# Sliding-window attention and SwiGLU block on one core: first values shifted half by DMA, two sums and the next keys issued at other places

## The chip, the core and the metric

The kernel runs on one core of one Trainium2 chip. The metric is the device time of one execution in microseconds (us). Before the change three runs took 337.42 us in the median (337.41 to 337.79).

## What is computed

Attention over a causal window of 64 positions, for 8 batches of 8 heads with 576 positions and head size 64; its output, 4608 tokens of 512 numbers, goes through a gated feed-forward block of width 1536.

```python
scores = scale * np.matmul(q, k.transpose(0, 1, 3, 2))      # 8 x 8 x 576 x 576
mask = (rel >= 0) & (rel < window)                          # window = 64
attn = softmax(where(mask, scores, -1e9))
x = np.matmul(attn, v).transpose(0, 2, 1, 3).reshape(4608, 512)
g = x @ w_gate                                              # 512 x 1536
silu = g * (1.0 / (1.0 + np.exp(-g)))
val = x @ w_val
return (silu * val @ w_out).astype(np.float32)              # 1536 x 512
```

Inputs and output are float32; the kernel multiplies in bf16.

## The kernel before, in words

The tokens are cut into nine tiles of 512 (t = 0 to 8). Tiles 0 to 6 and 8 are the first 512 positions of a batch; tile 7 gathers the last 64 positions of all eight. A tile passes through four stages.

- Scores (`scores`, L201): for each pair u of heads, small matmuls of 64 keys with the queries that can see them; `Exp` on ScalarE (L233) makes the weights E. For t = 0 the mask is added by matmuls with a bias (L219), later VectorE multiplies E with it (L235).
- Values: `totals` (L243) sums E with a matrix of ones into d_ps; ScalarE forms the inverse as exp(-log(d)), `log` at L253 and `invert` at L256. `values` (L265) multiplies E with v, 16 matmuls for a pair (L271), and VectorE scales the result into xT (L277).
- Gate (`gate_value`, L302): twelve steps m, each with eight matmuls of 512 columns (L306) into g_ps and v_ps; `gate_end` (L294) does silu on ScalarE (L299) and the product hT on VectorE (L300). For t = 0 the first two steps are done piece by piece by `gate_part` (L283, matmuls at L286), since each quarter c needs only the values of pair c.
- Projection (`project_part`, L312): twelve quarters of hT with wo (L315) into o_ps; VectorE copies it and SP stores it (L322, L325). Projection of tile t stands between the scores and values of tile t + 1.

The window of a 64-key block reaches over the boundary between two chunks of 128 positions. So v is kept twice: v1 has the chunks as they are, and v2 is shifted by 64 rows, with lower and upper half each on its own partitions. `shift_v` (L150) fills v2 from v1 with two copies per call: L155 copies the upper halves, L156 the lower. Its argument `copy` says who does it. For t = 0 it is called twice, for the chunks 0 and 1 and for 2 and 3, both times with VectorE (`on_v`). `values` takes v2 for even blocks and v1 for odd ones, in the order m = 0 to 7, so the first half of a pair's sixteen matmuls needs chunks 0 and 1, the second half chunks 2 and 3. For t >= 2 the shift is done with `shift_dma` (L401): SP starts a DMA from v1 to v2.

The order of the work is written out by hand: each engine executes its instructions in the order of the program text, and waits for what it reads. Around the change, it is this.

- Loads. SP starts the raw q and k of batch 0 and half of its v, ScalarE two quarters of k (L351 to L357). GpSimd starts everything that changes its type on the way: v chunks 2 and 3 of batch 0 (L430), the gate weights in five pairs (L442 to L447), q of batch 1 (L448, tile q_s), wo in three parts (L449 to L451), v of batch 1. Batch 1's keys are loaded raw (k_f) in four quarters by ScalarE's queue, L502, one after each of the gate steps m = 3 to 6. ScalarE casts a quarter (`join`, L505, instruction at L408) after the silu of m = 7 to 10, TensorE transposes it after the gate step m = 8 to 11 (L509, instruction at L174), and VectorE copies the result to kT (L510, instruction at L177). `turn_q` (L182, instruction at L186) turns batch 1's queries on VectorE, after m = 10, m = 11 and the loop.
- `keep_warm` (L366) issues matmuls on a tile of ones whose result nobody reads, seven at the start and a few later, six after `scores(0, 3)`.
- `log_of` (L465) does the sums and the log of one pair. Those of pairs 0 and 1 are done together (L455 to L460); pair 2's stand after the values of pairs 0 and 1, pair 3's between the two halves of the first gate pieces (L471 to L478).

Of the kernel before, what the change touches and what calls it, by code (L numbers as in the profile page):

```python
# [8 lines left out]
P = 128  # L9
# [8 lines left out]
def kernel(  # L18
# [10 lines left out]
    nc = tc.nc  # L29
    S, D, H = 576, 64, 8  # L30
# [23 lines left out]
    ones = cst.tile([P, 512], BF16, name="ones")  # L54
# [17 lines left out]
    def load_runs(eng, dst, src, t, hs):  # L72
        eng.dma_start(
            dst.rearrange("r h e d -> r h (e d)"),
            src[batch(t), hs, 0:512].rearrange("h (r e) d -> r h (e d)", e=4),
        )
# [73 lines left out]
    def shift_v(t, copy, lo=0, hi=4):  # L150

        a, b = v1[t % 2], v2[t % 2]
        top = min(hi, 3)
        if top > lo:
            copy(b[64:128, lo + 1:top + 1], a[64:128, lo:top])  # L155
        copy(b[0:64, lo:hi], a[0:64, lo:hi])  # L156
# [14 lines left out]
    def transposes(tp, src):  # L171

        for e in range(4):
            nc.tensor.transpose(tp[:, P * e:P * e + P], src[:, e], identb[:])  # L174

    def split_k(dst, tp):
        nc.vector.tensor_copy(  # L177
            dst.rearrange("p (r e) -> p r e", e=4),
            tp.rearrange("p (e r) -> p r e", e=4),
        )  # L180

    def turn_q(t, u):  # L182

        if u == 0:
            queries[t] = att.tile([P, 4, 512], BF16, name="qT", tag="qT")
        nc.vector.transpose(  # L186
            queries[t][:, u, :].rearrange("r (e x) -> r e x", e=16),
            staged[t][0][:, u].rearrange("r (e d) -> r e d", d=D)[:, :, 0:32],
        )
# [53 lines left out]
    def totals(t, u, d_ps):  # L243
        for h in range(2):
            nc.tensor.matmul(  # L245
                d_ps[64 * h:64 * h + 64], ones[:, 0:D], weights[t, u][:, h, :]
            )

    def room(n):
        return fsb.tile([P, 2, 512], FP32, name="r", tag="r", bufs=4)[:, 0:n]  # L250

    def log(r, d_ps):
        nc.scalar.activation(r, d_ps, AF.Ln)  # L253
# [11 lines left out]
    def values(t, u, o_ps):  # L265
        E = weights.pop((t, u))
        if u == 0:
            xT[t] = att.tile([P, 4, 512], BF16, name="xT", tag="xT")
        for m in range(8):
            for h in range(2):  # L270
                nc.tensor.matmul(  # L271
                    blocks(o_ps[64 * h:64 * h + 64], t, m, m + 1),
                    (v1, v2)[m // 4][t % 2][:, m % 4, 2 * u + h, :] if t == LAST
                    else (v2, v1)[m % 2][t % 2][:, m // 2, 2 * u + h, :],
                    blocks(E[:, h, :], t, m, m + 1),
                )
        nc.vector.tensor_mul(xT[t][:, u, :], o_ps[:], inverse.pop((t, u)))  # L277
# [5 lines left out]
    def gate_part(t, ms, tiles, c):  # L283
        for m, pair in zip(ms, tiles):
            for ps, w in zip(pair, (wg, wv)):
                nc.tensor.matmul(  # L286
                    ps[:], w[:, c, P * m:P * m + P], xT[t][:, c, :],
                    start=(c == 0), stop=(c == 3),
                )

    def gate_tiles():
        return [ps_f.tile([P, 512], FP32, name=x + "_ps", tag=x) for x in "gv"]

    def gate_end(t, m, pair):  # L294
        if m == 0:
            hT[t] = hpool.tile([P, 12, 512], BF16, name="hT", tag="hT")
        g_ps, v_ps = pair
        sg = fsb.tile([P, 512], FP32, name="sg", tag="sg")
        nc.scalar.activation(sg[:], g_ps[:], AF.Silu)  # L299
        nc.vector.tensor_mul(hT[t][:, m, :], sg[:], v_ps[:])  # L300

    def gate_value(t, m):  # L302
        pair = gate_tiles()
        for ps, w in zip(pair, (wg, wv)):
            for c in range(4):
                nc.tensor.matmul(  # L306
                    ps[:], w[:, c, P * m:P * m + P], xT[t][:, c, :],
                    start=(c == 0), stop=(c == 3),
                )
        gate_end(t, m, pair)  # L310
# [33 lines left out]
    def set_exp():  # L344
        nc.scalar.preload_act_table_set("natural_log_exp_and_others")
# [7 lines left out]
    for u in range(4):  # L353
        hs = slice(2 * u, 2 * u + 2)
# [1 line left out]
        load_runs(nc.scalar if u < 2 else nc.sync, raw[1][:, hs], k, 0, hs)  # L356
    load_v(nc.sync, staged[0, "v"], 0, (0, 1))  # L357
    set_exp()
    nc.vector.memset(ones[:], 1.0)
    make_identity(nc, identb[:])  # L360
    nc.vector.memset(zero[:], 0.0)
    for i in range(2):
# [1 line left out]
    warm = ps_f.tile([P, 512], FP32, name="warm", tag="v")  # L364

    def keep_warm(n):  # L366
        for _ in range(n):
            nc.tensor.matmul(warm[0:D], ones[:, 0:D], ones[:])

    keep_warm(7)  # L370
    nc.gpsimd.memset(tri[:], 1.0)
    for a in range(2):
        half = tri[64 * a:64 * a + 64]
# [25 lines left out]
    on_v, on_p, on_a = nc.vector.tensor_copy, nc.gpsimd.tensor_copy, nc.scalar.copy  # L399
# [7 lines left out]
    def join(copy, dst, src):  # L407
        copy(dst.rearrange("r e (h d) -> r h e d", h=2), src)  # L408

    def one(name):  # L410
        return ps_a.tile([P, 2, 512], FP32, name=name, tag="a")[:, 0]
# [48 lines left out]
    invert(r)  # L460
    scores(0, 3)
    shift_v(0, on_v, 0, 2)
    shift_v(0, on_v, 2, 4)

    def log_of(u):  # L465
        d_ps = one("d_ps")
        totals(0, u, d_ps)
        inverse[0, u] = room(1)[:, 0]
        log(inverse[0, u], d_ps)

    keep_warm(6)  # L471
    for u in range(2):
        values(0, u, ps_f.tile([P, 512], FP32, name="ao_ps", tag="gv"[u])[:])
    log_of(2)
    pairs = [gate_tiles() for _ in range(2)]
    gate_part(0, (0,), pairs, 0)
    log_of(3)
    gate_part(0, (1,), pairs[1:], 0)  # L478
    for u in (2, 3):
        invert(inverse[0, u])  # L480
    values(0, 2, one("ao_ps"))
# [6 lines left out]
    for m in range(12):  # L488
        if m < 2:
            gate_end(0, m, pairs[m])  # L490
        else:
            gate_value(0, m)
        if m == 2:
            for i in range(4):
                nc.vector.tensor_copy(
                    mask[:, 0, :, i], tri[:].rearrange("r c (x e) -> r e c x", e=16)
                )
            nc.vector.memset(mask[64:128, 0, :, 0, 0, :], 0.0)
            nc.vector.tensor_copy(mask[:, 1], mask[:, 0])
        if 3 <= m < 7:  # L500
            hs = slice(2 * m - 6, 2 * m - 4)
            load_runs(nc.scalar, raw_k[:, hs], k, 1, hs)  # L502
        if 7 <= m < 11:
            u = m - 7
            join(on_a, keys[:, u], raw_k[:, 2 * u:2 * u + 2])  # L505
        if m >= 8:
            u = m - 8
            tp = ps_a.tile([P, 512], BF16, name="tp", tag="a")
            transposes(tp, keys[:, u])  # L509
            split_k(kT[1][:, u, :], tp[:])  # L510
        if m >= 10:
            turn_q(1, m - 10)
    turn_q(1, 2)
    turn_q(1, 3)

    set_exp()
# [96 lines left out]
```

The softmax here doesn't subtract the row's maximum and nothing guards it: scores larger than these inputs give would overflow.

## Time and profile before

| | |
|---|---|
| median of three runs | 337.42 us |
| the profiled execution | 337.54 us, span 335.7 us |
| TensorE busy | 323.2 us, 96% of the span |
| VectorE, ScalarE, GpSimd busy | 214.2, 169.2, 137.8 us |
| first values (L271) | 13.93; second half of pair 0 from 14.99 |
| first gate matmul (L286) | 16.16 |
| first matmul of the gate step m = 2 (L306) | 21.29 |
| batch 1's scores, pair 0 and pair 1 (L227) | 39.94, 42.02 |
| first projection matmul (L315) | 42.38 |
| batch 1's first gate matmul (L306) | 56.29 |

Times in the lower rows are microseconds from the start of the span. The page gives each engine's busy time; the span in 40 slices of 8.4 us, with tenths of busy time for each engine and for the 16 DMA engines; and the DMA queues, of which q0 carries what GpSimd starts, q1 what SP starts and q10 what ScalarE starts. The chain of waits follows the work that ended last back from the end, and lists what released each step. The list of waits says for which releaser an engine stood idle. A window of the DMA view counts the packets of each queue in that stretch. A DMA's landing is the moment at which its semaphore tells that all of it is there.

### The profile page before, as it was taken

Reading aid. Unit: us, or ns where it says so; the run is one execution under the profiler, and the core shown is the slowest. Engines: PE = TensorE matmul, PEld = TensorE weight load, DVE = VectorE, ACT = ScalarE, POOL = GpSimd, SP = SyncE. Lnnn points to the kernel's source line nnn. Section 1 sums busy time; section 2 is a strip of 40 time slices with the busy share of each in tenths; the row PEclk is TensorE's granted clock in tenths of the full one; section 3 lists DMA queues with packets and bytes.
Section 4 is the critical chain, followed back from the end, with each engine's and each line's share of the span. In section 5 each row is a group of like instructions: output and inputs, shape, how many; then the busy total and the mean of one; then the engine's idle time right before and its main releaser. Section 6 shows DMA issues by size and latency. Waiting matters only on the chain.

```text
span 335.7 us, 6932 instructions
## 1 busy us (share of the span) xinstructions
PE 323.2 (96%) x2683; PEld 153.9 (46%) x2729; DVE 214.2 (64%) x318; ACT 169.2 (50%) x241; POOL 137.8 (41%) x247
## 2 busy tenths in 40 slices
PE   8899799999999999999999999999999999999994
PEld 3444344444544454445444544444444444544441
DVE  5754766588667756785678656865786476753431
ACT  4764656336733763366435553565347633763300
POOL 5944345946767965256123896163200000000000
PEclk9999999999999999999999999999999999999999
DMA  7999999999899499639931999199401320010013
GB/s 261 205 202 226 229 188 223 125 205 215 147 248 186 52 176 234 124 58 209 185 89 20 170 180 167 12 189 177 111 0 48 79 56 3 23 72 31 3 32 94
DMA packets 83057, 44.12 MB, mean 131 GB/s; under 512 B 63824, under 2 KB 77648, under 8 KB 83024
## 3 DMA queue, kind: packets, MB, share of 16 engines
q0 software_dynamic: 49328, 22.56, 54.2%
q1 hardware_dynamic: 31680, 19.02, 20.6%
q10 hardware_dynamic: 2016, 2.10, 2.2%
q8 instruction: 21, 0.34, 0.4%
q14 instruction: 12, 0.10, 0.1%
HBM read 54.00 MB, written 9.44 MB: 189 GB/s over the span
## 4 chain that ended last, share of the span: by engine, by line
PE 88%; DMA 6%; DVE 3%; issue 2%; ACT 1%; DVEq 0%
PE g_ps L306 26%; PE v_ps L306 26%; PE o_ps L315 25%; PE s_ps L227 3%; DMA k_f<-in_k_dram 3%; PE ao_ps L271 3%; PE d_ps L245 3%; DMA q_f<-in_q_dram 1%; PE tp L174 1%; PE g_ps L286 1%; ACT E L233 1%; DVE kT L177 1%; PE v_ps L286 1%; DMA out_dram<-os__4409 1%; DMA out_dram<-os__4428 1%
## 5 line engine op out<-in xcount | busy, mean ns | idle before, releaser
L299 ACT ACTIVATE sg<-g_ps 128x512 f32<-128x512 f32 x108 | 64.4, 597 | 112.1 <-PE g_ps L306 79.9
L300 DVE TENSOR_TENSOR hT<-sg,v_ps 128x512 bf16<-128x512 f32 x108 | 74.9, 694 | 62.9 <-PE v_ps L306 59.9
L306 PE MATMUL v_ps<-xT,wv 128*128 128x512 bf16 x417 | 108.3, 379 | 0.5
L306 PE MATMUL g_ps<-xT,wg 128*128 128x512 bf16 x413 | 107.6, 379 | 0.5
L315 PE MATMUL o_ps<-wo,hT 128*128 128x512 bf16 x405 | 96.5, 380 | 1.6 <-issue 0.6
L107 POOL DMA_DIRECT2D k_s<-in_k_dram x112 | 60.7, 551 | 29.8 <-DMA q_s<-in_q_dram 20.5
L306 PEld LDWEIGHTS <-wv 128*128 128x128 bf16 x424 | 41.5, 98 | 50.0
L306 PEld LDWEIGHTS <-wg 128*128 128x128 bf16 x424 | 41.4, 98 | 49.5 <-issue 0.3
L315 PEld LDWEIGHTS <-hT 128*128 128x128 bf16 x432 | 39.6, 98 | 45.1 <-issue 0.4
L233 ACT ACTIVATE E<-s_ps 128x1024 bf16<-128x1024 f32 x36 | 35.2, 1021 | 8.4 <-PE s_ps L227 8.2
L277 DVE TENSOR_TENSOR xT<-ao_ps,r 128x512 bf16<-128x512 f32 x36 | 24.7, 691 | 22.7 <-ACT r L256 20.5
L196 DVE STREAM_TRANSPOSE kT<-k_s 128x512 bf16<-128x512 bf16 x28 | 35.9, 1284 | 0.0
L253 ACT ACTIVATE r<-d_ps 128x512 f32<-128x512 f32 (+1 forms) x35 | 21.0, 601 | 22.4 <-PE d_ps L245 22.4
L235 DVE TENSOR_TENSOR E<-E,mask 128x1024 bf16<-128x1024 bf16 x28 | 20.5, 739 | 11.5 <-ACT E L233 11.5
L87 POOL DMA_DIRECT2D q_s<-in_q_dram x28 | 15.3, 558 | 26.7 <-DVE qT L186 16.0
L148 POOL CAST v<-v_f 128x512 bf16<-128x512 f32 x22 | 14.3, 665 | 21.5 <-DMA v_f<-in_v_dram 17.5
L256 ACT ACTIVATE r<-r 128x512 f32<-128x512 f32 (+1 forms) x35 | 22.3, 641 | 1.1
L186 DVE STREAM_TRANSPOSE qT<-q_s 128x512 bf16<-128x512 bf16 x32 | 22.3, 702 | 0.0
L271 PEld LDWEIGHTS <-v 128*64 128x64 bf16 x576 | 13.8, 112 | 5.7 <-issue 1.7
L271 PE MATMUL ao_ps<-E,v 128*64 128x64 bf16 x576 | 15.3, 196 | 0.6 <-DVE v L156 0.6
L245 PE MATMUL d_ps<-E,ones 128*64 128x512 bf16 x72 | 13.9, 392 | 0.3
L227 PE MATMUL s_ps<-qT,kT 64*64 64x128 bf16 (+1 forms) x640 | 12.5, 211 | 0.2 <-DVE kT L177 0.2
(95 smaller groups left out, 175.6 us busy)
## 6 DMA issues: line engine op xcount, KB each, us to landing
q_s<-in_q_dram POOLq DMA_DIRECT2D x28, 248.0 KB, 6.7
k_s<-in_k_dram POOLq DMA_DIRECT2D x112, 56.0 KB, 5.2
v_f<-in_v_dram SPq DMA_DIRECT2D x22, 256.0 KB
v<-in_v_dram POOLq DMA_DIRECT2D x18, 128.0 KB, 4.8
k_f<-in_k_dram ACTq DMA_DIRECT2D x6, 256.0 KB
wo<-in_moe_w_out_dram POOLq DMA_DIRECT2D x3, 512.0 KB, 16.0
v<-v SPq DMA_DIRECT2D x6, 256.0 KB
v<-v SPq DMA_DIRECT2D x6, 192.0 KB
```

Source lines behind the costliest of these rows:

```text
L107: nc.gpsimd.dma_start(k_s[p0:p0 + 32, g, :, 0:w], k[b, a:H:2, s:s + P].rearrange("u (r e) d -> r u (e d)", e=4) [:, :, 32 * c:32 * c + w],)
L186: nc.vector.transpose(queries[t][:, u, :].rearrange("r (e x) -> r e x", e=16), staged[t][0][:, u].rearrange("r (e d) -> r e d", d=D)[:, :, ...
L196: nc.vector.transpose(dst[:, u, :].rearrange("r (g x e) -> r g e x", g=4, e=4), k_s[:, :, u].rearrange("r g (e d) -> r g e d", d=D)[:, :, ...
L227: nc.tensor.matmul(blocks(s_ps[64 * c:64 * c + 64, h], t, lo, hi), zero[r] if src is None else src[r, u, x:x + 64], blocks(qT[r], t, lo, h ...
L233: nc.scalar.activation(E[:], s_ps[:], AF.Exp, scale=0.125)
L245: nc.tensor.matmul(d_ps[64 * h:64 * h + 64], ones[:, 0:D], weights[t, u][:, h, :])
L271: nc.tensor.matmul(blocks(o_ps[64 * h:64 * h + 64], t, m, m + 1), (v1, v2)[m // 4][t % 2][:, m % 4, 2 * u + h, :] if t == LAST else (v2, v ...
L277: nc.vector.tensor_mul(xT[t][:, u, :], o_ps[:], inverse.pop((t, u)))
L299: nc.scalar.activation(sg[:], g_ps[:], AF.Silu)
L300: nc.vector.tensor_mul(hT[t][:, m, :], sg[:], v_ps[:])
L306: nc.tensor.matmul(ps[:], w[:, c, P * m:P * m + P], xT[t][:, c, :], start=(c == 0), stop=(c == 3),)
L315: nc.tensor.matmul(o_ps[:], hT[t][:, c, P * s:P * s + P], wo[:, c, :], start=(c == 0), stop=(c == 11),)
```

## The change

Four edits:

- the memset of the ones is cut in two, so that the first 128 columns come alone; the seven warm matmuls at the start become six of 128 columns and six of 512;
- the shift of chunks 2 and 3 for t = 0 is done by two DMAs on SP's queue, instead of two copies on VectorE;
- pair 2's sums and log stand ahead of the values of pairs 0 and 1, pair 3's directly behind them and ahead of the gate pieces, which then come in one call; one of six warm matmuls is dropped;
- batch 1's keys are loaded after the gate steps m = 1 to 4 instead of 3 to 6, cast after m = 5 to 8 instead of 7 to 10, transposed after m = 6 to 9 instead of 8 to 11; the queries are turned after m = 9, 10, 11 and the loop.

```diff
-    nc.vector.memset(ones[:], 1.0)
+    nc.vector.memset(ones[:, 0:P], 1.0)
+    nc.vector.memset(ones[:, P:512], 1.0)
...
-    keep_warm(7)
+    for _ in range(6):
+        nc.tensor.matmul(warm[0:D, 0:P], ones[:, 0:D], ones[:, 0:P])
+    keep_warm(6)
...
     shift_v(0, on_v, 0, 2)
-    shift_v(0, on_v, 2, 4)
+    shift_v(0, shift_dma, 2, 4)
...
-    keep_warm(6)
+    keep_warm(5)
+    log_of(2)
     for u in range(2):
         values(0, u, ps_f.tile([P, 512], FP32, name="ao_ps", tag="gv"[u])[:])
-    log_of(2)
+    log_of(3)
     pairs = [gate_tiles() for _ in range(2)]
-    gate_part(0, (0,), pairs, 0)
-    log_of(3)
-    gate_part(0, (1,), pairs[1:], 0)
+    gate_part(0, (0, 1), pairs, 0)
...
-        if 3 <= m < 7:
-            hs = slice(2 * m - 6, 2 * m - 4)
+        if 1 <= m < 5:
+            hs = slice(2 * m - 2, 2 * m)
             load_runs(nc.scalar, raw_k[:, hs], k, 1, hs)
-        if 7 <= m < 11:
-            u = m - 7
+        if 5 <= m < 9:
+            u = m - 5
             join(on_a, keys[:, u], raw_k[:, 2 * u:2 * u + 2])
-        if m >= 8:
-            u = m - 8
+        if 6 <= m < 10:
+            u = m - 6
             tp = ps_a.tile([P, 512], BF16, name="tp", tag="a")
             transposes(tp, keys[:, u])
             split_k(kT[1][:, u, :], tp[:])
-        if m >= 10:
-            turn_q(1, m - 10)
-    turn_q(1, 2)
+        if m >= 9:
+            turn_q(1, m - 9)
     turn_q(1, 3)
```

## The prediction

> **What bounds the kernel now.** I read the page first, then TensorE's waits over the whole span, then the chain and the DMA windows of the first 58 us, which the change touches.
>
> ```profile
> PE 323.2 (96%) x2683; PEld 153.9 (46%) x2729; DVE 214.2 (64%) x318; ACT 169.2 (50%) x241; POOL 137.8 (41%) x247
> ...
> DMA  7999999999899499639931999199401320010013
> ```
>
> TensorE sets the end, and the DMA engines are full in the first six slices (8.4 us each). The chain after 56.5 us is gate, projection and attention matmuls with hardly a break, so what the first 57 us gain or lose reaches the end. These are TensorE's waits, in us in total, times, longest:
>
> ```profile
> PE s_ps L227 <- DVE qT L186: 1.7, 1, 1.7
> ...
> PE ao_ps L271 <- DVE v L156: 0.6, 1, 0.6
> ...
> PE g_ps L286 <- DVE xT L277: 0.4, 1, 0.4
> ```
>
> So there is little to win: 1.7 us where batch 1's scores wait for a turned query, 1.0 us around the first values. The chain shows what lies behind the first values (start, us, what):
>
> ```profile
> 12.37 0.77 DVE v L155
> 13.13 0.01 issue
> 13.15 0.73 DVE v L156
> 13.87 0.03 issue
> 13.90 0.58 DVE v L155
> 14.48 0.03 issue
> 14.51 0.43 DVE v L156
> 14.94 0.04 issue
> 14.99 0.33 PE ao_ps L271 x8
> ```
>
> VectorE's four copies (L155, L156) make the shifted values; the last two are those that the change gives to SP. And behind batch 1's scores:
>
> ```profile
> 29.26 9.63 DMA k_f<-in_k_dram
> ...
> 39.44 0.60 ACT sg L299
> ...
> 40.66 0.68 DVE kT L177
> 41.35 0.63 DVE qT L186
> ```
>
> The last quarter of batch 1's keys takes 9.63 us to arrive; the cast, the last silu, a key copy and a query turn stand one behind the other, and TensorE waits 1.66 us until 42.02.
>
> **What the skill says.** (1) "DMA: Bandwidth & Descriptors", section on the anatomy of one DMA: about 2.0 us fixed plus bytes at 436 GB/s. For 128 KB that is an estimate of 2.3 us. This trace's loaded queue is far from it: a k_f quarter needs 7.6 to 9.6 us. (2) The same page, section on queues, rings and completion order: an engine goes round-robin between the queues that it has work for, packet by packet. The trace agrees in steady state (32 to 36 us: 423 packets of q0, 426 of q10), but not for the first packet, which comes late; this decides the case. (3) "TensorE: Matmul & The Clock Gate", Part 1: after about 3.4 us of idleness the clock falls to half. The waits here are up to 1.7 us and the page shows full clock after the start; no run here shows a longer one.
>
> **Part 1: the second half of the shift by DMA.** Removed from VectorE: 0.58 + 0.43 us and the gaps, from 13.87 to 14.94. Added: two DMAs on SP's queue, 64 KB and 128 KB, each behind the landing of one chunk of v. Nothing else stands on SP's queue until 48.97, so nobody there is delayed. The chunks are issued by GpSimd at 6.33 and about 7.3 and land 4.8 to 5.0 us later: 11.3 and 12.15. From then the question is when a hardware DMA gets through beside GpSimd's backlog. Two windows (4 us each) tell; first 24 to 28 us, then 28 to 32:
>
> ```profile
> q0 software_dynamic: 1269, 0.80, 136.4%
> q10 hardware_dynamic: 4, 0.00, 0.4%
> ```
>
> ```profile
> q0 software_dynamic: 360, 0.61, 80.9%
> q10 hardware_dynamic: 348, 0.34, 30.7%
> ```
>
> The k_f load was issued at 24.08, and only 4 packets moved before 28.0: 3.9 us to the first. After that 87 packets a us. The later shift (v<-v at 66.12) moves no packet before 70.0, about 4 us too. Here: issue 11.3, first packets at 15.2, then 64 packets of 1 KB (0.6 us) and 64 of 2 KB (0.6 us), and the receipt, 0.2. All shifted values are there at T = 16.6. Bounds: unloaded 12.15 + 2.3 = 14.4; as slow as the later shift, whose 128 packets are through only between 72 and 73, 12.15 + 6.6 = 18.7. TensorE meets this in order: values of pair 0 need both DMAs in their second half, and everything on TensorE is queued behind them. VectorE's freed 1.0 us is worth nothing, since its next work is xT, behind the same values. So T = 16.6 takes the place of 14.94.
>
> **Part 2: the sums.** Pair 2's sums go ahead of the values, and one warm matmul (0.22) is dropped for them: nothing on the path, TensorE is waiting there. Pair 3's sums (0.34 of the chain) leave the middle of the gates for the place after values of pairs 0 and 1; its exp ends at 15.11, before T, so it costs no wait and lies under the xT product. From the values' release to the first gate: 16.16 - 14.99 = 1.18, kept. From the first gate to L306's first matmul (m = 2): 21.29 - 16.16 = 5.13, less 0.34 and about 0.12 of switching: 4.67. ScalarE's logs and inverses come sooner (inverse of pair 2 by T + 2.2, needed at T + 2.8), so no new wait. m = 2 starts at T + 0.04 + 1.18 + 4.67 = T + 5.89 = 22.49, against 21.29: 1.2 later. This stretch alone breaks even at T = 15.4.
>
> **Part 3: keys two steps sooner.** Moved on ScalarE: four issues (0.37 each, on its sequencer), from the silus of m = 3 to 6 to m = 1 to 4, and four casts (0.62) from m = 7 to 10 to m = 5 to 8. Moved on TensorE: 16 transposes, four per step (0.22 to 0.25 a step); on VectorE: four key copies (0.68), with the first query turns (0.70) from m = 10 to m = 9. With today's latencies (7.6, 8.8, 9.2, 9.6) and issues at 22.4, 23.55, 25.3, 27.0 they land at 30.0, 32.4, 34.5, 36.6; the casts are due at 29.3, 31.1, 32.8, 34.5, so ScalarE still waits, and transposes lose at most 0.2 each, like now. But after m = 9 two steps follow without a cast: VectorE does qT 0 and 1 by about 40.8 under the gates of m = 10 and 11 (0.69 + 0.70 of a 1.73 step), and the second scores find it done. From m = 2 to the first scores now 39.94 - 21.29 = 18.65; ideal is 10 x 1.727 + 4 x 0.25 = 18.27; I take 18.4. Then 0.83 for two score groups instead of 42.38 - 39.94 = 2.44. First projection matmul: 22.49 + 18.4 + 0.83 = 41.72 against 42.38: 0.66 sooner.
>
> What comes late next is wo. Its three loads land 15.7 to 16.9 us after issue: 39.7, 42.3, 44.7. The shift adds 192 KB, about 0.5 us at the 385 GB/s that plain loads reach (4 to 6 us), so 40.2, 42.8, 45.2. The keys come ahead of the q_s and wo data, but all of them did by 38.9 anyway. Needed: 41.7; eight matmuls later, 43.5; then, after the second block's first four, 46.0. Hidden by 0.7 us or more. q_s (landing by 36.5, with the keys ahead about 37.7) is needed at 38.7. Gate weights were 2 us or more ahead and lose at most 1.
>
> **Part 4: warm-up.** Seven matmuls at 0.427 spacing (2.99 us from 1.53) become six of 128 columns (0.10 to 0.2) and six of 512, starting some 0.3 sooner: end at 4.4 to 5.0 against 4.52, where the transposes wait for a cast until 4.79. Between 0.1 gained and 0.2 lost, and either way covered by T: I take nothing. If T were early, this cover would be gone and 0.2 could show.
>
> **Sum.** Profiled execution 337.54 (span 335.7): minus 0.66 is 336.9. The median is 0.12 below that execution, so 336.8.
>
> **Rivals.** All use first projection at T + 25.12, so break-even is T = 17.26, and 0.1 us of T is 0.1 us of time; 0.2% of 337.42, about what a measurement tells from no change, is 0.67 us.
>
> A, forecast: T between 16.0 and 17.3: 336.2 to 337.5. For it: 3.9 and about 4 us to the first packet in two places.
>
> B, the DMA comes through quickly (T = 14.4). Then pair 3's exp (15.11) holds the gates, m = 2 is at about 20.3 and projection could start at 39.5; wo takes over, whose last third at 45.2 plus eight matmuls (1.78) ends the block at 47.0 instead of 48.43: gain 1.4, 336.0. For it: the queue at 11.3 is shallower than at 24. Against it: DMA engines are full, and 0.5 MB of weights are already issued.
>
> C, slower: the shift waits as the later one did, T = 18.7: 1.4 later than break-even, 338.9. It loses from T = 17.3 on, by over 0.2% from T = 17.95. TensorE idles from 14.4 to T; at 4.3 us the clock gate could halve the next 3.4 us and add up to 1.7: 340.5. Speaking for it: the trace's own shift took 6.6. Against: there a software packet took 112 ns (106.4% of 16 engines' 4 us over 610 packets), at 14 to 18 us it takes 59 (143.6%, 1548).
>
> D, sooner keys don't remove the wait: they and the weights delay each other, and q_s or a cast comes so late that 1.66 us of waiting stays. Then part 1's loss is bare: 338.5. Against it: the turn has 1.9 us of spare steps.
>
> **How the numbers follow.** A 0.50, half of it beyond 0.67 us: faster 0.25, same 0.25. B 0.18, faster. C 0.22, slower 0.20, same 0.02. D 0.10, slower 0.07, same 0.03. Together faster 0.43, same 0.30, slower 0.27. The range runs from B's 336.0 less 0.2 for a wo that isn't delayed, 335.8, to C without the clock, 338.9: it leaves out some 0.1 above and 0.05 below. A's own is 336.2 to 337.5.
>
> **What would show it.** TensorE's wait before ao_ps on a v<-v DMA, 2.2 us, ended at 16.6; m = 2 at 22.5; no wait of s_ps for qT; o_ps from 41.7; no wait for wo. I am wrong in part 1 if the values go on before 15.5 or after 17.3, in part 3 if s_ps still waits for qT or L306 stops for weights, and in the rest if the clock falls.

## The result, and the profile after

The changed kernel takes 340.93 us in the median of four runs (339.85 to 341.18), the kernel before 337.61 us beside it (337.41 to 337.98): a ratio of 1.0091, 95% interval 1.0067 to 1.0115. It is 0.9% slower, beyond the upper end of the range. The profiled execution takes 341.18 us, its span is 339.1.

Two rows of the 40 slices (8.4 us each) on the page of the kernel before, TensorE's busy tenths and the tenths of its clock that were granted:

```profile
PE   8899799999999999999999999999999999999994
...
PEclk9999999999999999999999999999999999999999
```

and the same rows of the kernel after (8.5 us each):

```profile
PE   8579999999999999999999999999999999999994
...
PEclk9959999999999999999999999999999999999999
```

TensorE's share of busy time is 96% in both. The loss is in the second and third slices: TensorE's second slice is 5 instead of 8, and its clock in the third slice is 5, where it was 9 before. TensorE's two longest waits in the first 60 us of the kernel after (total, times, longest):

```profile
PE ao_ps L271 <- DMA v<-v: 4.6, 1, 4.6
PE warm L372 <- DVE ones L359: 1.1, 1, 1.1
```

The wait for qT is gone, as was meant, and so is the one for VectorE's copies. One wait of 4.6 us on the shift DMA stands in their place. The chain of the kernel after shows its parts (start, us, what):

```profile
7.13 5.59 DMA v<-in_v_dram
...
12.73 5.61 DMA v<-v
...
18.39 0.85 PE ao_ps L271 x14
```

Chunk 3 of v takes 5.59 us to land, and the shift DMA that waits for it takes 5.61 more. The last line shows the other part of the loss: the matmuls that follow take 0.85 us. The timeline of before has 0.57 for the same 24 matmuls:

```profile
14.99 0.57 PE L271 MATMUL ao_ps<-E,v 128*64 128x64 bf16 x24 [0.65 <-DVE v L156]
```

The windows from 13 to 18.4 and from 18.4 to 26.4 us of the kernel after show why; after the five engines' busy times comes the granted clock, then the DMA share and GB/s:

```profile
13.00:18.40 5.40, 0.76 (x14) 0.41 (x10) 0.00 (x0) 2.02 (x3) 4.73 (x7) 0.94 1.42 212
18.40:26.40 8.00, 7.66 (x73) 3.51 (x75) 2.67 (x4) 3.52 (x6) 2.94 (x5) 0.61 1.32 203
```

TensorE works 0.76 of 5.4 us, and right after that, until 26.4, it runs at 0.61 of its clock on average.

Milestones of the two profiled executions, us from the span's start, and what each stretch adds:

| stretch on TensorE | before | after | change |
|---|---|---|---|
| start to the second half of pair 0's values | 14.99 | 18.39 | +3.40 |
| from there to m = 2 (L306) | 6.30 | 8.06 | +1.76 |
| m = 2 to the first projection matmul (L315) | 21.09 | 19.49 | -1.60 |
| first projection to batch 1's first gate matmul | 13.91 | 13.91 | 0.00 |
| from there to the end | 279.4 | 279.3 | -0.1 |
| span | 335.7 | 339.1 | +3.4 |

### The profile page after: what moved, and what is told of

The parts are those of the page before. It is cut to its first block, busy times and chain, and to the rows that moved or that the text cites. A ratio compares the mean times of both kernels' runs of the same rounds, so it can differ in the third digit from the quotient of the medians.

```text
span 339.1 us, 6944 instructions
## 1 busy us (share of the span) xinstructions
PE 324.5 (96%) x2687; PEld 154.5 (46%) x2733; DVE 212.2 (63%) x317; ACT 169.1 (50%) x241; POOL 137.3 (40%) x247
## 3 DMA queue, kind: packets, MB, share of 16 engines
q1 hardware_dynamic: 31840, 19.21, 20.8%
## 4 chain that ended last, share of the span: by engine, by line
PE 86%; DMA 9%; issue 1%; DVE 1%; ACT 1%; POOL 0%; SPq 0%; POOLq 0%
PE g_ps L306 25%; PE v_ps L306 25%; PE o_ps L315 25%; PE ao_ps L271 3%; PE s_ps L227 3%; PE d_ps L245 3%; DMA k_f<-in_k_dram 3%; DMA v<-v 2%; DMA v<-in_v_dram 2%; DMA q_f<-in_q_dram 1%; PE v_ps L286 1%; PE g_ps L286 1%; ACT E L233 1%; DMA out_dram<-os__4395 1%; DMA out_dram<-os__4414 1%
## 5 line engine op out<-in xcount | busy, mean ns | idle before, releaser
L306 PE MATMUL v_ps<-xT,wv 128*128 128x512 bf16 x416 | 108.2, 379 | 0.5
L306 PE MATMUL g_ps<-xT,wg 128*128 128x512 bf16 x414 | 107.8, 379 | 0.4
L315 PE MATMUL o_ps<-wo,hT 128*128 128x512 bf16 x405 | 96.5, 380 | 1.7 <-issue 0.6
L306 PEld LDWEIGHTS <-wv 128*128 128x128 bf16 x424 | 41.5, 98 | 50.0
L306 PEld LDWEIGHTS <-wg 128*128 128x128 bf16 x424 | 41.3, 98 | 49.3 <-issue 0.3
L315 PEld LDWEIGHTS <-hT 128*128 128x128 bf16 x432 | 39.5, 98 | 45.1 <-issue 0.4
L87 POOL DMA_DIRECT2D q_s<-in_q_dram x28 | 15.2, 553 | 30.9 <-DVE qT L186 18.0
L235 DVE TENSOR_TENSOR E<-E,mask 128x1024 bf16<-128x1024 bf16 x28 | 19.8, 708 | 10.1 <-ACT E L233 9.8
L271 PE MATMUL ao_ps<-E,v 128*64 128x64 bf16 x576 | 16.5, 200 | 4.6 <-DMA v<-v 4.6
L271 PEld LDWEIGHTS <-v 128*64 128x64 bf16 x576 | 14.6, 116 | 10.6 <-DMA v<-v 4.8
```

The source lines that it names most:

```text
L271: nc.tensor.matmul(blocks(o_ps[64 * h:64 * h + 64], t, m, m + 1), (v1, v2)[m // 4][t % 2][:, m % 4, 2 * u + h, :] if t == LAST else (v2, v ...
L306: nc.tensor.matmul(ps[:], w[:, c, P * m:P * m + P], xT[t][:, c, :], start=(c == 0), stop=(c == 3),)
L315: nc.tensor.matmul(o_ps[:], hT[t][:, c, P * s:P * s + P], wo[:, c, :], start=(c == 0), stop=(c == 11),)
```

## The experiments

Theory: the shift DMA comes late because it waits while the DMA engines work on what GpSimd has already handed to them (most of the +3.4; chunk 3 of v itself landed 0.6 later than before), and TensorE's idle stretch then costs it half its clock (+2.2 within the second row, where the moved sums give back 0.44). Rivals: the sums or the keys have a cost of their own; the clock falls for another reason or costs nothing; a DMA from v1 to v2 is slow in itself.

**The shift back on VectorE** (an edit of the kernel after):

```diff
-    shift_v(0, shift_dma, 2, 4)
+    shift_v(0, on_v, 2, 4)
```

> The changed kernel with the second half of the shift back on VectorE; the other three edits stay. Theory (the wait for the two shift DMAs, and the half clock after it, cost all that was lost): the values go on at 14.3 to 14.9, the clock stays full, m = 2 starts 5.9 later at 20.2 to 20.8, pair 1's scores don't wait for qT; 1.2 to 1.9 us faster than before, 335.7 to 336.4 beside 337.6, with wo as the limit of the gain. Rival (the sooner keys or the moved sums have a cost of their own): 337.5 or more.

Measured: 336.34 us, ratio to before 0.9960 (0.9946 to 0.9974), clock 1.000. The second half of pair 0's values goes on at 14.40 as expected, 4.0 us sooner than in the kernel after. One line turns 0.9% slower into 0.4% faster, so the other three edits together show no cost. But two things differ from the expectation: m = 2 starts at 20.85, just after the 20.8 that it named, and pair 1's scores still wait 0.3 us for qT. TensorE's waits in the first 60 us of this kernel:

```profile
PE o_ps L315 <- DMA wo<-in_moe_w_out_dram: 0.7, 1, 0.7
...
PE v_ps L286 <- DMA wv<-in_moe_w_val_dram: 0.4, 1, 0.4
...
PE s_ps L227 <- DVE qT L186: 0.3, 1, 0.3
```

and the line of its timeline where the longest of them ends:

```profile
42.89 1.02 PE L315 MATMUL o_ps<-wo,hT 128*128 128x512 bf16 x4 [0.67 <-DMA wo<-in_moe_w_out_dram]
```

Now weights are late: wv of the first gate piece by 0.4, wo by 0.7. The wait of 0.7 is for the second third of wo, since only eight matmuls (two for each of the first four quarters) stand before it and the projection started at 40.31. The last third lands at 45.5 and costs a wait of only 0.1.

**The shift DMA alone** (an edit of the kernel before):

```diff
-    shift_v(0, on_v, 2, 4)
+    shift_v(0, shift_dma, 2, 4)
```

> The kernel before with only the second half of the shift given to SP's DMA queue. Theory: values go on at about 18.3 instead of 14.9, TensorE is idle for over 4 us, the clock falls to half for some 7 us, m = 2 at about 26.8 instead of 21.3; 341.5 to 343. Rival (the loss comes from the moved sums or keys, not from the shift): within 0.5 us of before, 337.6.

Measured: 342.24 us, ratio 1.0135 (1.0107 to 1.0163), clock 0.987. The values go on at 17.97, after a wait of 3.7 us where the theory had over 4:

```profile
17.97 0.85 PE L271 MATMUL ao_ps<-E,v 128*64 128x64 bf16 x24 [3.66 <-DMA v<-v]
```

m = 2 starts at 26.46, and a wait of 1.5 us for qT is left. The second edit alone makes more than the whole loss; the other edits take 0.4% of it back.

**Warm matmuls in the wait** (an edit of the kernel after):

```diff
     keep_warm(5)
     log_of(2)
+    keep_warm(18)
```

> The changed kernel with 18 more warm matmuls (3.9 us at full clock) ahead of the first values, where TensorE waits. Theory (of the 3.3 us lost, some 2.2 are the half clock that the idle stretch brings): values still go on at about 18.3, but the clock stays full, mean 0.998, and m = 2 starts 5.9 later at about 24.3; 338.5 to 339.2. Rival (the clock falls for another reason, or costs nothing): 340.5 to 341.

Measured: 338.61 us, ratio 1.0026 (1.0013 to 1.0038), clock 0.999. The window from 13 to 18.2 us and the one from the values' release to m = 2:

```profile
13.00:18.20 5.20, 4.92 (x32) 2.48 (x28) 0.47 (x1) 2.30 (x3) 4.75 (x8) 1.00 1.42 211
18.20:24.10 5.90, 5.28 (x74) 2.65 (x76) 2.71 (x5) 3.58 (x6) 2.11 (x4) 1.00 1.33 205
```

and the line of the timeline where the values go on:

```profile
18.23 0.57 PE L271 MATMUL ao_ps<-E,v 128*64 128x64 bf16 x24 [0.31 <-DMA v<-v]
```

The values come no sooner (18.23 against 18.39), but 4.92 of 5.2 us are filled with work that nobody reads, and the clock is 1.00 afterwards. From the release to m = 2 it takes 5.86 us instead of 8.06. So 2.20 us of the loss were the lowered clock, by the profiles; the medians say 340.93 - 338.61 = 2.3. What is left, 1.0 us over before, is the late DMA less what the other edits gain.

**The keys alone**: the fourth edit on the kernel before.

```diff
-        if 3 <= m < 7:
+        if 1 <= m < 5:
...
-        if 7 <= m < 11:
+        if 5 <= m < 9:
...
-        if m >= 8:
+        if 6 <= m < 10:
...
-        if m >= 10:
+        if m >= 9:
```

> The kernel before with only the fourth edit, batch 1's keys two gate steps sooner. Theory: m = 2 as before at 21.3, pair 1's scores don't wait for qT, first projection matmul 1.4 to 1.8 sooner; 335.9 to 336.3. Rival (the keys still come late, as their loads compete with the weights, and the wait only changes its place): 337.2 to 337.6.

Measured: 336.19 us, ratio 0.9954 (0.9937 to 0.9970). The wait for qT is gone, m = 2 is at 21.41, and the first projection matmul comes at 40.26 instead of 42.38, 2.1 sooner where 1.4 to 1.8 were expected; 1.1 sooner is left at batch 1's first gate matmul (55.17 for 56.29). The waits for wo tell where most of the difference goes, 0.25 us for its second third at 42.41 and 0.43 for its last:

```profile
45.42 0.81 PE L315 MATMUL o_ps<-wo,hT 128*128 128x512 bf16 x2 [0.43 <-DMA wo<-in_moe_w_out_dram]
```

The stretch between the two is 14.91 us long, 1.0 more than before, and 0.7 of it is these two waits. This edit alone gives as much as the three together (336.19 and 336.34 us can't be told apart); in both profiles TensorE waits 0.7 us for wo.

**No backlog ahead of the shift** (an edit of the kernel after):

```diff
+    idle = cst.tile([P, 512], FP32, name="idle")
...
-    weights_gv(0, 256)
     cast_v(0, (0, 1))
+    for _ in range(9):
+        nc.gpsimd.tensor_copy(idle[:], ones[:])
+    weights_gv(0, 256)
     weights_gv(256, 512)
```

> The changed kernel with GpSimd's gate weights issued only after nine dummy copies, so that no weights are queued when the two shift DMAs are issued. The computation is whole, but the weights come some 6 us later, so only the landing of the shift is read, not the time. Theory (the shift waits for what GpSimd's queue has already handed to the DMA engines): the last shift DMA is through 2.3 to 3.2 us after its issue, instead of 5.6. Rival (the DMA from v1 to v2 is slow in itself): 5 us or more.

Measured, in one execution: the second half of the values goes on at 14.67, with SP's issue at 12.2:

```profile
14.67 0.57 PE L272 MATMUL ao_ps<-E,v 128*64 128x64 bf16 x24 [0.62 <-DMA v<-v]
```

The DMA windows of this kernel, 12 to 13 and 13 to 15 us; q0, GpSimd's queue, moves nothing in them:

```profile
q1 hardware_dynamic: 80, 0.07, 28.5%
```

```profile
q1 hardware_dynamic: 80, 0.13, 28.6%
```

Beside them the kernel after, 12 to 14, 14 to 16, 16 to 17 and 17 to 19 us; in the first of these q1 moves nothing, though its two DMAs were issued at 11.7 and 12.7:

```profile
q0 software_dynamic: 774, 0.38, 144.0%
```

```profile
q0 software_dynamic: 710, 0.35, 130.9%
q1 hardware_dynamic: 76, 0.06, 9.8%
```

```profile
q0 software_dynamic: 376, 0.19, 139.1%
q1 hardware_dynamic: 11, 0.02, 5.1%
```

```profile
q0 software_dynamic: 665, 0.33, 121.7%
q1 hardware_dynamic: 73, 0.12, 17.2%
```

The same 64 KB and 128 KB (64 data packets and 16 closing ones each). Without weights in the queue the second DMA needs 2.4 us from its issue to the values; with them 5.6. The estimate of 2.3 us, on which the prediction's lower bound rests, comes from the Trainium skill's fit in "DMA: Bandwidth & Descriptors", the section on the anatomy of one DMA. The page gives this fit for DMAs that GpSimd starts; here it comes out for one that SP starts, on empty queues. The rival that the DMA is slow in itself falls. What sets the length of the wait is not shown: this run takes away the backlog and every other load of the DMA engines at once, and no run varies the backlog's size. The execution takes 343.74 us, since TensorE then waits 5.5 us for wg:

```profile
20.98 0.61 PE L287 MATMUL g_ps<-xT,wg 128*128 128x512 bf16 x1 [5.52 <-DMA wg<-in_moe_w_gate_dram]
```

So delaying the weights is no way out.

**When the clock falls.** Three of these kernels have a lowered clock after a wait. Their windows from 17 to 18 us, the kernel after first, then the shift DMA alone, then the kernel without backlog, have TensorE nearly or wholly idle:

```profile
17.00:18.00 1.00, 0.00 (x0) 0.00 (x0) 0.00 (x0) 0.00 (x0) 0.73 (x1) 0.90 1.32 249
```

```profile
17.00:18.00 1.00, 0.03 (x2) 0.03 (x3) 0.00 (x0) 0.00 (x0) 0.45 (x1) 0.57 1.45 198
```

```profile
17.00:18.00 1.00, 0.00 (x0) 0.00 (x0) 0.00 (x0) 0.98 (x2) 1.00 (x3) 0.73 0.00 0
```

The window before shows 1.00 in each, the next one 0.50. If the clock steps from 1.00 to 0.50 once in the window, it fell at 17.8, 17.1 and 17.5 (0.90 is 0.2 us of half clock, 0.57 is 0.86 and 0.73 is 0.54). The waits began at 13.8, 14.3 and 15.5, the time at which TensorE went on less the wait. So the fall came about 4.0, 2.8 and 2.0 us after the start of a wait. In the last case TensorE had also stood idle for 0.6 us shortly before, until 14.67.

**The sums alone**: the third edit on the kernel before (`log_of(2)` ahead of the values, `log_of(3)` behind them, the gate pieces in one call, `keep_warm(5)`).

> The kernel before with only the third edit, the sums of pairs 2 and 3 where their exps end and one warm matmul less. Theory: m = 2 0.3 to 0.5 sooner, and pair 1's scores still wait for qT; 337.0 to 337.3. Rival (the wait for the last quarter of the keys takes it back): 337.5 to 337.7.

Measured: 337.24 us, ratio 0.9987 (0.9976 to 0.9998). A gain, if a small one, within the expected range. m = 2 starts at 20.22, 1.1 us sooner where 0.3 to 0.5 were expected (the next run comes back to this), and the wait for qT grows to 1.8 us in total.

**The warm-up alone**: the first edit on the kernel before.

> The kernel before with only the first edit, the ones set in two steps and six narrow and six wide warm matmuls at the start. Theory from the runs so far: the full clock is granted at 4 to 5 us instead of 6.9, the scores of batch 0 end some 0.5 us sooner, and the first values too; 336.9 to 337.4. Rival (the prediction's: nothing of it reaches the path): 337.5 to 337.7.

Measured: 337.52 us, ratio 0.9995 (0.9980 to 1.0009): no difference can be told, as the rival said. Its profiled execution is ahead by 0.6 us at m = 2 (20.69), but so is that of the sums alone, by 1.1 (20.22), of which their edit explains only 0.44. The first matmuls with a bias show where more of it lies; first the kernel before, then the sums alone:

```profile
6.32 0.64 PE L219 MATMUL s_ps<-bias,identb 64*64 64x512 bf16 x4
```

```profile
5.93 0.41 PE L219 MATMUL s_ps<-bias,identb 64*64 64x512 bf16 x4
```

Up to here these two kernels have the same program, and yet the same four matmuls take 0.64 us in one execution and 0.41 in the other: the moment at which TensorE comes to its full pace varies. In three of the four profiles without the first edit they take 0.64, in all six with it 0.41. The edit may help there, but one execution of each is too little to say so, and the medians show no gain.

**A later need for wo** (the kernel after, with the shift on VectorE):

```diff
         if u % 2:
-            project_part(0, (0, 1), halves, range(3 * u - 3, 3 * u + 3))
-    for s in range(2):
-        project_end(0, s, halves[s])
+            project_part(0, (0, 1), halves, range(3 * u - 3, 6 if u == 1 else 8))
...
     for u in range(2):
         sums(1, u, d_tile())
+    for s in range(2):
+        project_part(0, (s,), halves[s:s + 1], range(8, 12))
+        project_end(0, s, halves[s])
+    for i in range(4):
+        shift_v(1, on_v, i, i + 1)
```

> The changed kernel with the shift on VectorE, and the last third of wo needed later: after six quarters and the scores of pairs 2 and 3 only two more quarters are multiplied, then the sums of batch 1's pairs 0 and 1, then the last four quarters, one output tile after the other. Theory (wo's landing at 45.4 now limits the gain, with 0.7 us of waiting): the wait falls below 0.3, 0.3 to 0.7 us faster than with VectorE's shift alone, 335.6 to 336.0. Rival (the wait goes to the copy of the output tile or to v, which lands just after): 336.3.

Measured: 336.04 us, ratio 0.9946 (0.9924 to 0.9967). This has the lowest median of all, 0.3 us below VectorE's shift alone, but the intervals overlap: faster than before by 0.5% is shown, faster than the first experiment is not. The expectation also had the wait in the wrong place. In the first experiment the 0.7 us were for the second third of wo, and this edit moves only the need for the last. What is left here is again the second third:

```profile
42.37 1.02 PE L315 MATMUL o_ps<-wo,hT 128*128 128x512 bf16 x4 [0.32 <-DMA wo<-in_moe_w_out_dram]
```

It was issued at 27.96 instead of 28.55 and landed 0.5 sooner, which the edit doesn't explain, and the wait for qT rose from 0.3 to 0.8. So this run doesn't show what a later need for wo is worth.

## Why the prediction was wrong, step by step

**Part 1 is the step that failed: "All shifted values are there at T = 16.6."** They went on at 18.39. Two terms were too small. Chunk 3 of v landed at 12.72 instead of 12.15; it took 5.6 us from its issue here and about 4.9 before. And the second DMA took 5.6 us instead of 4.45: I had its packets follow the first one's without a new wait. The windows above show otherwise. The first DMA's packets move from 14 us on, sooner than the 15.2 that I had taken; then come 11 packets in a microsecond, and the bulk of the second only after 17, some 4 us after its own issue at 12.7. So the wait of 3.9 us was near the truth for the second DMA, but it ran from that DMA's issue and not from the first one's. The upper bound that I had taken from the later shift, 18.7, was the right end to take.

**The second step that failed is a term put at nothing in the forecast: the clock.** I held the price of a long idle stretch in rival C, where it was added to 340.5, and kept it out of the forecast and of the range because no run here showed it. Even there it was too small, at most 1.7 us for 2.2 measured. It is this term that takes the result out of the range: with the DMA as late and the clock kept, the run with warm matmuls took 338.61 us, which the range still held. The two errors together close the sum: (18.34 - 17.26) + 2.20 = 3.28 us, for 3.32 between the medians.

The Trainium skill, "TensorE: Matmul & The Clock Gate", Part 1, puts the fall after about 3.4 us of idleness. The traces differ: the clock fell 4.0, 2.8 and 2.0 us into three waits, as shown above, so less than 3.4 us of one wait can be enough. With 18 matmuls in the same wait the clock stayed, so that it is the idle time, and that it costs 2.2 us, is shown.

From what length on a wait can lower the clock is not shown. The 1.7 us wait of the kernel before left the clock whole in its profiled execution. But three kernels without a shift by DMA have a wait of 1.4 to 1.7 us for qT: before, the sums alone and the warm-up alone. Of their executions that were measured with the experiments, 30 of 122 show a mean clock of 0.992 to 0.994 and 338.1 us or more. In four kernels that wait is gone or below 1 us and no other long one stands in its place: the first experiment, the warm matmuls, the keys alone and the later need for wo. Of their executions none of 48 does. So it may be that this wait, too, lowers the clock now and then, and that the sooner keys are worth more than the medians say; no such execution was profiled, and this is not shown. The price of the long wait varies too: one of the four executions of the kernel after had a mean clock of 0.995 and took 339.85 us, the others 0.988 or 0.989 and 340.88 or more.

Rival C is what happened in kind: T = 18.3 for 18.7, and 340.93 for 338.9 to 340.5. I gave it 0.22. The evidence that I set against it, shorter packets in the backlog, was a guess on how a queue's turn is counted; the trace had one shift of the same kind under load, at 6.6 us, and one k_f load at 3.9 to the first packet, which I took as the whole delay.

**Part 2 was right.** From the values' release to m = 2 it named 5.89 - 0.04 = 5.85; with the clock kept it is 5.86. Alone it gives 0.13%, 0.4 us.

**Part 3 was right in its mechanism and near in size.** From m = 2 to the first projection it named 18.4 + 0.83 = 19.23; it took 19.49 in the kernel after, and 19.25 in the run with warm matmuls in the wait. The k_f casts still wait, 3.8 us in total on ScalarE for 3.5 before, and it does not matter, as argued, because two steps without a cast follow. What is late next was named too: wo. In the kernel after it never shows, since all is 3.6 us later; in the three versions with the sooner keys and without the shift by DMA TensorE waits 0.3 to 0.7 us for it. "Hidden by 0.7 us or more" held for a start of the projection at 41.7; from 40.3 it is a wait.

**Part 4** was costed at nothing, and the medians show nothing.

## What to carry to other kernels

A small DMA issued while another queue has a backlog can't be priced by its bytes: here 128 KB took 2.4 us with nothing else under way and 5.6 with three weight loads of 256 KB under way (issued from 8.6 to 11.7, landed from 15.1 to 18.4), more than the 1.0 us of VectorE copies that it was to save. A wait in front of TensorE can have a second price beside its length, here in waits of 3.7 us and more (the fall itself came as early as 2.0 us into one). Such a wait is worth filling with dummy matmuls if it can't be shortened, and a forecast that holds one should carry the fallen clock in its main case. When edits are bundled, run them apart: three of the four were harmless or good, and part of what the sooner keys gain goes into a wait for the next transfer, wo.

## What the runs showed that I had not expected

Two DMAs of one queue, issued 1.0 us apart, came through far apart: the first had 76 of its 80 packets through by 16, the second most of its own only after 17.

The lowered clock outlasted its cause: in the kernel after it held for about 6.9 us (0.06 x 2 x 5.4 + 0.39 x 2 x 8.0 from the two windows, if it is either full or half), although TensorE was busy for 7.66 of the last 8.0. With the shift DMA alone it held for about as long, from 17.1 to 24.0 us by its windows. Why it takes so long to come back was not tried.

The load of v's chunk 3, which no edit touches, took 4.8 us to land in the run without backlog and 5.6 in the kernel after. It also took 5.6 with the shift back on VectorE, so it is not the shift DMA that slowed it; what did was not tried.
